# Soft-capped attention ahead of two expert layers: value products of 64 columns, and the sums of the exponentials by additions and one product

## The chip, the core and the metric

The kernel runs on one core of one Trainium2 chip. The metric is the device time of one execution in microseconds, the median of several runs. A profile is taken of one further execution; its span runs from the first to the last instruction. TensorE, VectorE, ScalarE, GpSimd and SyncE are the five engines; the profile calls them PE (PEld for its weight loads), DVE, ACT, POOL and SP, and SPq is SyncE's queue of transfers.

## What is computed

For 2 batches of 12 heads, 448 positions and 64 columns a head:

```
s = (q @ k.T) / sqrt(64)
s = cap * tanh(s / cap)              # cap = 30
a = exp(s - max(s)); a = a / (sum(a) + 1e-9)
x = a @ v                            # heads side by side: 896 tokens x 768
h = x @ w_in;  x = relu(h)**2 @ w_out
h = x @ w_in2; out = (h * clip(h + 3, 0, 6) / 6) @ w_out2
```

Where the cap is at most 40, as here, the kernel leaves the maximum out, since the exponentials can't overflow. It divides after the product with v: the numerator is the product of v and the exponentials, the denominator their sum over the keys.

## The kernel before, in words

There are 12 pairs of heads. Scores are computed transposed, keys on the partitions and the 448 queries along the columns. The 448 keys of a head are three tiles of 128 and a rest of 64; a step handles one key tile g of both heads of a pair: g = 1, 2, 3 the full ones, g = 0 the rest, for which the two heads share the 128 partitions. The stream of 48 steps goes pair by pair in the order `TILES` = 1, 2, 3, 0.

At step t the loop of L362 writes down, in this order, the work of several steps, and each engine takes its own in that order: `scores` (L274: two float32 products of 64 rows, one a head, on the two halves of TensorE's rows), `squash` (L286: ScalarE's tanh out of PSUM, both heads at once), `powers` of the step before (L293: ScalarE's exponential in place) and `weigh` of three steps before (L297, `LAG`). `weigh` multiplies the exponentials by a weight tile of 128 columns: 64 columns of v and 64 of ones, so that one product per head gives numerators in 64 partitions of a bank and, in each of the other 64, the sum. A float32 product shows in the trace as two records.

After a pair's last `weigh`: `evict` copies both banks out on VectorE (L318), and SyncE moves one row of sums for each head to 64 partitions (L319); `invert` adds the guard and takes reciprocals (L324, L325) and SyncE stores the result to DRAM (L327); `spread` has it broadcast to 64 partitions for each head (L333); `divide` multiplies on GpSimd (L340); `part` splits the quotient into a hi part in the fp32r type (GpSimd, L48, for the last pair ScalarE, L46) and a lo part (VectorE, L349), which the expert layers take as `xh` and `xl`. Each of these follows some steps behind the one before. `load` fetches q and k (L234) and v (L272, two transfers a pair into three fixed tiles) three pairs ahead, on SyncE, which issues all transfers in program order and waits where a transfer has to wait.

Spread over the loop, the first three chunks of expert weights are prepared (`split_steps`, five steps a chunk, on GpSimd and VectorE, then the next load, L81). After the loop `begin` starts the first two products of the expert layers (L134): first all that needs batch 0, then batch 1 without the last pair, 66 products in all, and only then what needs the last pair. The expert layers follow on TensorE, three products for each block (hi by hi, hi by lo, lo by hi). Scores take two tiles of two PSUM banks each (`ps_a`), numerators four banks (`ps_o`).

Of the kernel before, what the change touches and what calls it, by code (L numbers as in the profile page):

```python
# [9 lines left out]
F32 = mybir.dt.float32  # L10
# [6 lines left out]
PSUM = bass.MemoryType.PSUM  # L17

B, H, S, D = 2, 12, 448, 64
DM, DFF = 768, 2048  # L20
P = 128
NQ = S // P
REM = S - NQ * P
HP = H // 2
NPAIR = B * HP
# [4 lines left out]
OCH = 4  # L30
NO = KF // OCH
RC = S // D
TILES = (1, 2, 3, 0)
LAG = 3
EPS = 1e-9
SAFE_CAP = 40.0
SAFE_BITS = 0x42200000
# [199 lines left out]
def attention(tc, ex, qk, v, loaded, sc, capt, guard, set_guard):  # L237
# [6 lines left out]
    nc = tc.nc  # L244
    with ExitStack() as actx:
        dram = actx.enter_context(tc.tile_pool(name="dram", bufs=2, space=bass.MemoryType.DRAM))
        a1 = actx.enter_context(tc.tile_pool(name="a1", bufs=1))
        a2 = actx.enter_context(tc.tile_pool(name="a2", bufs=2))
        a3 = actx.enter_context(tc.tile_pool(name="a3", bufs=3))
        a5 = actx.enter_context(tc.tile_pool(name="a5", bufs=5))  # L250
        ps_o = actx.enter_context(tc.tile_pool(name="ps_o", bufs=4, space=PSUM))

        pairs = [{} for _ in range(NPAIR)]
        pairs[0].update(loaded)


        v3 = []
        for i in range(3):
            t = a1.tile([P, NQ + 1, 3, D], F32, name=f"v{i}")
            nc.gpsimd.memset(t[:, :, 1, :], 1.0)  # L260
            v3.append(t)

        def load(p):
            if p >= NPAIR:
                return
            t = pairs[p]
            if p > 0:
                t["qk"] = a3.tile([P, 2, S], F32, name="qk", tag="qk")
                load_qk(nc, t["qk"], qk[p])
            t["v"] = v3[p % 3]  # L270
            for h in range(2):
                nc.sync.dma_start(t["v"][:, :, 2 * h, :], v[p, :, :, h])  # L272

        def scores(p, g):  # L274
            t = pairs[p]
            st = t["st", g] = ex.sums()
            for h in range(2):
                rows = slice(h * D, (h + 1) * D)
                if g:

                    out, c0, n = st[:, h, :S], h * REM + (g - 1) * P, P
                else:
                    out, c0, n = st[rows, 0, :S], (1 - h) * (S - REM), REM
                nc.tensor.matmul(out, t["qk"][rows, 1, c0:c0 + n], t["qk"][rows, 0, :], start=True, stop=True)  # L284

        def squash(p, g):  # L286
            t = pairs[p]
            n = 2 if g else 1
            e = a5.tile([P, 2, S], F32, name="e", tag="e")
            t["e", g] = e[:, :n, :]  # L290
            nc.scalar.activation(t["e", g], t.pop(("st", g))[:, :n, :S], AF.Tanh, scale=sc)  # L291

        def powers(p, g):  # L293
            e = pairs[p]["e", g]
            nc.scalar.activation(e, e, AF.Exp, scale=capt)  # L295

        def weigh(p, g):  # L297
            t = pairs[p]
            e = t.pop(("e", g))
            for h in range(2):  # L300
                if g == TILES[0]:
                    t["po", h] = ps_o.tile([P, 512], F32, name="po", tag="po")
                rows = slice(0, P) if g else slice(h * D, (h + 1) * D)
                w = t["v"][rows, g - 1 if g else NQ, h:h + 2, :].rearrange("p a d -> p (a d)")
                nc.tensor.matmul(  # L305
                    t["po", h][:, :S], w, e[rows, h if g else 0, :],
                    start=g == TILES[0], stop=g == TILES[-1],
                )

        def evict(p):
            t = pairs[p]
            t["ev"] = a2.tile([P, 2, S], F32, name="ev", tag="ev")
            t["rec"] = a2.tile([D, 2, RC], F32, name="rec", tag="rec")
            for h in range(2):
                s0 = (1 - h) * D
                nc.vector.tensor_copy(t["ev"][:, h, :], t.pop(("po", h))[:, :S])  # L318
                nc.sync.dma_start(t["rec"][:, h, :], t["ev"][s0:s0 + 1, h, :].rearrange("o (p c) -> o p c", c=RC))  # L319

        def invert(p):
            t = pairs[p]
            rec = t["rec"]
            nc.vector.tensor_scalar_add(rec, rec, guard[:D])  # L324
            nc.vector.reciprocal(rec, rec)  # L325
            t["rows"] = dram.tile([2, S], F32, name="rows", tag="rows")
            nc.sync.dma_start(t["rows"].rearrange("h (p c) -> p h c", c=RC), rec)  # L327

        def spread(p):
            t = pairs[p]  # L330
            t["rb"] = a2.tile([P, S], F32, name="rb", tag="rb")
            for h in range(2):
                nc.sync.dma_start(t["rb"][h * D:(h + 1) * D], t["rows"][h:h + 1].to_broadcast([D, S]))  # L333

        def divide(p, eng):
            t = pairs[p]
            t["xf"] = a2.tile([P, S], F32, name="xf", tag="xf")
            for h in range(2):
                x = slice(h * D, (h + 1) * D)
                eng.tensor_mul(t["xf"][x], t["ev"][x, h, :], t["rb"][x])  # L340

        def part(p, i, eng):
            xf = pairs[p]["xf"]
            b, hp = divmod(p, HP)
            at = (slice(None), hp, slice(b * S, (b + 1) * S))
            if i == 0:
                copy(nc, eng, ex.xh[at], xf)
            else:
                eng.tensor_sub(ex.xl[at], xf, ex.xh[at].bitcast(F32))  # L349

        load(0)
        set_guard()
        load(1)
        load(2)
        ex.load()
        ex.load()
        stream = [(p, g) for p in range(NPAIR) for g in TILES]
        n, m = len(stream), len(TILES)
        early = (s for w in ("pvp",) * 3 for s in ex.split_steps(w))
        after = {m * (p + 1) - 1 + LAG: p for p in range(NPAIR)}  # L360

        for t in range(n + LAG + 5):  # L362
            if t < n:
                scores(*stream[t])
                squash(*stream[t])
            if 1 <= t <= n:
                powers(*stream[t - 1])
            if LAG <= t < n + LAG:
                weigh(*stream[t - LAG])
            if t in after:  # L370
                evict(after[t])
                load(after[t] + 3)
            if t - 5 in after:
                part(after[t - 5], 1, nc.vector)
            if t - 2 in after:
                invert(after[t - 2])
            if t - 3 in after:
                spread(after[t - 3])
            if t - 4 in after and after[t - 4] < NPAIR - 1:
                divide(after[t - 4], nc.gpsimd)  # L380
                part(after[t - 4], 0, nc.gpsimd)
            elif t - 4 in after:
                divide(after[t - 4], nc.vector)
                part(after[t - 4], 0, nc.scalar)
            if t >= 3 and t % 2:
                next(early, None)
            if t == n:
                for _ in early:
                    pass
        begun = ex.begin([ex.sums() for _ in range(2)])  # L390
        part(NPAIR - 1, 1, nc.vector)
        for _ in begun:
# [144 lines left out]
```

## Time and profile before

| what | value |
|---|---|
| median of 3 runs | 607.37 us (606.34 to 607.92) |
| the profiled execution | 604.25 us, span 602.5 us |
| mean granted TensorE clock | 0.994 of full speed |
| TensorE busy | 587.0 us of the span |
| VectorE, ScalarE, GpSimd busy | 313.3, 276.5 and 156.0 us |
| transfers | 65.14 MB, mean 108 GB/s |

Busy times are shares of one long span with two parts, attention and expert layers, so they don't tell what bounds either; that is read from the timeline. A group of instructions on one line has a count, the busy time, the mean of one, and the idle time of its engine ahead of it with what ended it. In a timeline, consecutive records of a line stand together (x4: four records), with the start and the time to the end of the last; ends on TensorE are modelled, so the distance from start to start tells more than the length.

### The profile page before, as it was taken

What the parts mean: (1) busy time and instruction counts of PE and PEld (TensorE: products, weight loads), DVE (VectorE), ACT (ScalarE), POOL (GpSimd) and SP (SyncE); (2) the same over time, 40 slices, a digit from 0 to 9 for tenths busy, and PEclk for the clock granted to TensorE, in tenths of its full rate; (3) what the DMA queues carried; (4) which work ended last, traced back from release to release, by engine and by line L of the source; (5) the groups of instructions that cost most, each with busy time, mean ns of one, the idle gap of its engine ahead of it and who ended that gap; (6) DMA issues with size and microseconds to landing.
All of it is one profiled execution on the core that took longest, in us unless ns stands there. A gap on an engine that the chain in (4) does not pass through costs nothing.

```text
span 602.5 us, 7241 instructions
## 1 busy us (share of the span) xinstructions
PE 587.0 (97%) x2688; PEld 477.2 (79%) x2688; DVE 313.3 (52%) x423; ACT 276.5 (46%) x434; POOL 156.0 (26%) x123
## 2 busy tenths in 40 slices
PE   6999999997999999999999999999999999999996
PEld 2333333376999999999999999999999999999995
DVE  0333232216766665555555567777777665554430
ACT  6767676705656665422333234555554432222220
POOL 0053433231322222222322232222222132222220
PEclk9999999998999999999999999999999999999998
DMA  7463636102433322234333443333332234433411
GB/s 172 140 157 87 166 77 165 34 17 72 153 106 107 109 92 97 71 106 138 106 105 95 133 156 108 104 106 104 106 110 85 87 104 137 135 115 127 146 57 36
DMA packets 35133, 65.14 MB, mean 108 GB/s; under 512 B 18704, under 2 KB 24848, under 8 KB 35088
## 3 DMA queue, kind: packets, MB, share of 16 engines
q1 hardware_dynamic: 34944, 64.59, 35.4%
q8 instruction: 23, 0.38, 0.2%
q14 instruction: 22, 0.18, 0.1%
q10 hardware_dynamic: 144, 0.00, 0.0%
HBM read 61.74 MB, written 2.80 MB: 107 GB/s over the span
## 4 chain that ended last, share of the span: by engine, by line
PE 81%; DMA 10%; POOL 3%; DVE 2%; issue 1%; SPq 1%; ACT 0%; POOLq 0%; ACTq 0%
PE pm L134 76%; DMA rows<-rec 4%; DMA rb<-rows 4%; PE po L305 3%; POOL xf L340 3%; PE pm L284 3%; DMA qk<-in_qk_dram 1%; DMA rec<-ev 1%; DMA qkfirst<-in_qk_dram 1%; POOL xh L48 1%; SPq L333 0%; DVE rec L325 0%; SPq L319 0%; DVE rec L324 0%; DVE xl L349 0%
## 5 line engine op out<-in xcount | busy, mean ns | idle before, releaser
L108 POOL TENSOR_TENSOR wl<-wv,wh 128x512 fp32r<-128x512 f32 (+1 forms) x80 | 121.2, 1516 | 340.6 <-ACT wh L46 335.7
L98 DVE TENSOR_SCALAR wv<-wy 128x512 uint32<-128x512 uint32 (+1 forms) x80 | 89.8, 1122 | 110.8 <-ACT wy L46 96.5
L134 PE MATMUL pm<-gh,wl 128*128 128x448 f32 x384 | 140.2, 365 | 0.0
L134 PE MATMUL pm<-gl,wh 128*128 128x448 f32 x384 | 140.2, 365 | 0.0
L134 PE MATMUL pm<-gh,wh 128*128 128x448 f32 x384 | 140.2, 365 | 0.0
L46 ACT ACTIVATE wh<-wv 128x512 fp32r<-128x512 f32 (+1 forms) x77 | 54.8, 711 | 106.9 <-PE pm L134 74.4
L134 PEld LDWEIGHTS pm<-gh,wh 128*128 128x128 f32 x384 | 72.1, 188 | 5.7
L134 PEld LDWEIGHTS pm<-gl,wh 128*128 128x128 f32 x384 | 72.1, 188 | 5.7
L134 PEld LDWEIGHTS pm<-gh,wl 128*128 128x128 f32 x384 | 72.1, 188 | 5.7
L134 PE MATMUL pm<-xh,wh 128*128 128x448 f32 x192 | 71.1, 370 | 3.3 <-ACT xh L46 3.3
L305 PE MATMUL po<-e,v 128*128 128x448 f32 (+1 forms) x192 | 74.2, 558 | 0.0
L134 PE MATMUL pm<-xl,wh 128*128 128x448 f32 x192 | 71.0, 370 | 1.0 <-DVE xl L349 1.0
L134 PE MATMUL pm<-xh,wl 128*128 128x448 f32 x192 | 70.8, 369 | 0.0
L134 PE MATMUL pm<-yh,wh 128*128 128x448 f32 x192 | 70.1, 365 | 0.0
L134 PE MATMUL pm<-yl,wh 128*128 128x448 f32 x192 | 70.1, 365 | 0.0
L134 PE MATMUL pm<-yh,wl 128*128 128x448 f32 x192 | 70.1, 365 | 0.0
L100 DVE SCALAR_TENSOR_TENSOR wv<-wr,wv 128x512 uint32<-128x512 uint32 (+1 forms) x80 | 63.8, 798 | 2.7
L102 DVE SCALAR_TENSOR_TENSOR wv<-wy,wv 128x512 uint32<-128x512 uint32 (+1 forms) x80 | 63.7, 796 | 2.6
L305 PEld LDWEIGHTS po<-e,v 128*128 128x128 f32 (+1 forms) x192 | 29.1, 188 | 41.6 <-issue 30.1
L291 ACT ACTIVATE e<-pm,sc 128x896 f32<-128x896 f32 (+1 forms) x48 | 43.8, 911 | 32.2 <-PE pm L284 32.2
L46 ACT ACTIVATE wy<-wr 128x512 f32<-128x512 f32 (+1 forms) x77 | 56.9, 739 | 1.8 <-DMA wr<-in_wo_dram 1.6
L295 ACT ACTIVATE e<-e,capt 128x896 f32<-128x896 f32 (+1 forms) x48 | 45.0, 940 | 0.0
(45 smaller groups left out, 512.7 us busy)
## 6 DMA issues: line engine op xcount, KB each, us to landing
wr<-in_wi_dram SPq DMA_DIRECT2D x32, 768.0 KB, 4.4
wr<-in_wo_dram SPq DMA_DIRECT2D x48, 512.0 KB, 3.5
qk<-in_qk_dram SPq DMA_DIRECT2D x22, 224.0 KB, 3.8
v<-in_v_dram SPq DMA_DIRECT2D x24, 128.0 KB, 3.7
rb<-rows SPq DMA_DIRECT2D x24, 112.0 KB, 2.8
out_dram<-o SPq DMA_DIRECT2D x12, 224.0 KB, 2.0
qkfirst<-in_qk_dram SPq DMA_DIRECT2D x2, 224.0 KB, 4.1
rec<-ev SPq DMA_DIRECT2D x24, 1.8 KB, 2.2
```

The costliest lines, as they stand in the source:

```text
L46: eng.activation(dst, src, AF.Copy, scale=scale)
L48: eng.tensor_scalar(dst, src, scale, 1.0, op0=ALU.mult, op1=ALU.mult)
L98: nc.vector.tensor_scalar(w, y, 3, None, op0=ALU.logical_shift_left)
L100: nc.vector.scalar_tensor_tensor(w, low, 29, w, op0=ALU.logical_shift_right, op1=ALU.bitwise_or)
L102: nc.vector.scalar_tensor_tensor(w, y, 0x80000000, w, op0=ALU.bitwise_and, op1=ALU.bitwise_or)
L108: by[2].tensor_sub(l, w.bitcast(F32), h.bitcast(F32))
L134: self.nc.tensor.matmul(ps[:, b, :S], w[:, k - k0, :], a[:, k, b * S:(b + 1) * S], start=(k == 0 and w is wh and a is ah), stop=(k == nk - ...
L284: nc.tensor.matmul(out, t["qk"][rows, 1, c0:c0 + n], t["qk"][rows, 0, :], start=True, stop=True)
L291: nc.scalar.activation(t["e", g], t.pop(("st", g))[:, :n, :S], AF.Tanh, scale=sc)
L295: nc.scalar.activation(e, e, AF.Exp, scale=capt)
L305: nc.tensor.matmul(t["po", h][:, :S], w, e[rows, h if g else 0, :], start=g == TILES[0], stop=g == TILES[-1],)
L340: eng.tensor_mul(t["xf"][x], t["ev"][x, h, :], t["rb"][x])
```

## The change

Value products get weight tiles of 64 columns (v alone), one product for each head, into the two halves of the partitions of one bank instead of two banks. The exponentials of a pair's key tiles are added up on VectorE (`add`), and one product per head with a tile of ones (`total`) sums the result over the partitions, in a bank of its own, into 64 equal rows. `evict` copies only these sums. `divide` is one VectorE instruction that reads the numerators from PSUM; the hi part is on ScalarE for all pairs. A pair's v comes in one transfer. The loop now goes by rounds of one pair, with the work of neighbouring rounds written between.

```diff
@@ -247,18 +245,16 @@
         a1 = actx.enter_context(tc.tile_pool(name="a1", bufs=1))
         a2 = actx.enter_context(tc.tile_pool(name="a2", bufs=2))
         a3 = actx.enter_context(tc.tile_pool(name="a3", bufs=3))
-        a5 = actx.enter_context(tc.tile_pool(name="a5", bufs=5))
-        ps_o = actx.enter_context(tc.tile_pool(name="ps_o", bufs=4, space=PSUM))
+        a4 = actx.enter_context(tc.tile_pool(name="a4", bufs=4))
+        a8 = actx.enter_context(tc.tile_pool(name="a8", bufs=8))
+        ps_o = actx.enter_context(tc.tile_pool(name="ps_o", bufs=3, space=PSUM))
+        ps_t = actx.enter_context(tc.tile_pool(name="ps_t", bufs=1, space=PSUM))
 
...
-        v3 = []
-        for i in range(3):
-            t = a1.tile([P, NQ + 1, 3, D], F32, name=f"v{i}")
-            nc.gpsimd.memset(t[:, :, 1, :], 1.0)
-            v3.append(t)
+        halves = [slice(h * D, (h + 1) * D) for h in range(2)]
+        ones = a1.tile([P, D], F32, name="ones")
+        nc.gpsimd.memset(ones, 1.0)
 
         def load(p):
             if p >= NPAIR:
@@ -267,15 +263,13 @@
             if p > 0:
                 t["qk"] = a3.tile([P, 2, S], F32, name="qk", tag="qk")
                 load_qk(nc, t["qk"], qk[p])
-            t["v"] = v3[p % 3]
-            for h in range(2):
-                nc.sync.dma_start(t["v"][:, :, 2 * h, :], v[p, :, :, h])
+            t["v"] = a4.tile([P, NQ + 1, 2, D], F32, name="v", tag="v")
+            nc.sync.dma_start(t["v"], v[p])
 
...
         def squash(p, g):
             t = pairs[p]
             n = 2 if g else 1
-            e = a5.tile([P, 2, S], F32, name="e", tag="e")
-            t["e", g] = e[:, :n, :]
+            t["e", g] = a8.tile([P, 2, S], F32, name="e", tag="e")[:, :n, :]
             nc.scalar.activation(t["e", g], t.pop(("st", g))[:, :n, :S], AF.Tanh, scale=sc)
 
         def powers(p, g):
@@ -296,27 +289,44 @@
 
         def weigh(p, g):
             t = pairs[p]
-            e = t.pop(("e", g))
-            for h in range(2):
-                if g == TILES[0]:
-                    t["po", h] = ps_o.tile([P, 512], F32, name="po", tag="po")
-                rows = slice(0, P) if g else slice(h * D, (h + 1) * D)
-                w = t["v"][rows, g - 1 if g else NQ, h:h + 2, :].rearrange("p a d -> p (a d)")
+            if "po" not in t:
+                t["po"] = ps_o.tile([P, 512], F32, name="po", tag="po")
+            for h, half in enumerate(halves):
+                rows, at = (slice(0, P), h) if g else (half, 0)
                 nc.tensor.matmul(
-                    t["po", h][:, :S], w, e[rows, h if g else 0, :],
-                    start=g == TILES[0], stop=g == TILES[-1],
+                    t["po"][half, :S], t["v"][rows, g - 1 if g else NQ, h, :], t["e", g][rows, at, :],
+                    start=g == 1, stop=g == 0,
                 )
 
 
+        def add(p, g, eng):
+            t = pairs[p]
+            if g == 2:
+                t["es"] = a2.tile([P, 2, S], F32, name="es", tag="es")
+                eng.tensor_add(t["es"], t["e", 1], t["e", 2])
+            elif g:
+                eng.tensor_add(t["es"], t["es"], t["e", g])
+            else:
+                for h, half in enumerate(halves):
+                    eng.tensor_add(t["es"][half, h, :], t["es"][half, h, :], t["e", 0][half, 0, :])
+
+        def total(p):
+            t = pairs[p]
+            t["pt"] = ps_t.tile([P, 512], F32, name="pt", tag="pt")
+            for h, half in enumerate(halves):
+                nc.tensor.matmul(t["pt"][half, :S], ones, t["es"][:, h, :], start=True, stop=True)
+
+
 
         def evict(p):
             t = pairs[p]
-            t["ev"] = a2.tile([P, 2, S], F32, name="ev", tag="ev")
+            t["tot"] = a2.tile([P, S], F32, name="tot", tag="tot")
+            nc.vector.tensor_copy(t["tot"], t.pop("pt")[:, :S])
             t["rec"] = a2.tile([D, 2, RC], F32, name="rec", tag="rec")
             for h in range(2):
-                s0 = (1 - h) * D
-                nc.vector.tensor_copy(t["ev"][:, h, :], t.pop(("po", h))[:, :S])
-                nc.sync.dma_start(t["rec"][:, h, :], t["ev"][s0:s0 + 1, h, :].rearrange("o (p c) -> o p c", c=RC))
+                nc.sync.dma_start(
+                    t["rec"][:, h, :], t["tot"][h * D:h * D + 1, :].rearrange("o (p c) -> o p c", c=RC)
+                )
 
         def invert(p):
             t = pairs[p]
@@ -329,15 +339,13 @@
         def spread(p):
             t = pairs[p]
             t["rb"] = a2.tile([P, S], F32, name="rb", tag="rb")
-            for h in range(2):
-                nc.sync.dma_start(t["rb"][h * D:(h + 1) * D], t["rows"][h:h + 1].to_broadcast([D, S]))
+            for h, half in enumerate(halves):
+                nc.sync.dma_start(t["rb"][half], t["rows"][h:h + 1].to_broadcast([D, S]))
 
         def divide(p, eng):
             t = pairs[p]
             t["xf"] = a2.tile([P, S], F32, name="xf", tag="xf")
-            for h in range(2):
-                x = slice(h * D, (h + 1) * D)
-                eng.tensor_mul(t["xf"][x], t["ev"][x, h, :], t["rb"][x])
+            eng.tensor_mul(t["xf"], t.pop("po")[:, :S], t["rb"])
 
         def part(p, i, eng):
             xf = pairs[p]["xf"]
@@ -348,45 +356,50 @@
             else:
                 eng.tensor_sub(ex.xl[at], xf, ex.xh[at].bitcast(F32))
 
+        def on(p, step, *args):
+            if 0 <= p < NPAIR:
+                step(p, *args)
+
         load(0)
         set_guard()
         load(1)
         load(2)
         ex.load()
         ex.load()
-        stream = [(p, g) for p in range(NPAIR) for g in TILES]
-        n, m = len(stream), len(TILES)
         early = (s for w in ("pvp",) * 3 for s in ex.split_steps(w))
-        after = {m * (p + 1) - 1 + LAG: p for p in range(NPAIR)}
-
-        for t in range(n + LAG + 5):
-            if t < n:
-                scores(*stream[t])
-                squash(*stream[t])
-            if 1 <= t <= n:
-                powers(*stream[t - 1])
-            if LAG <= t < n + LAG:
-                weigh(*stream[t - LAG])
-            if t in after:
-                evict(after[t])
-                load(after[t] + 3)
-            if t - 5 in after:
-                part(after[t - 5], 1, nc.vector)
-            if t - 2 in after:
-                invert(after[t - 2])
-            if t - 3 in after:
-                spread(after[t - 3])
-            if t - 4 in after and after[t - 4] < NPAIR - 1:
-                divide(after[t - 4], nc.gpsimd)
-                part(after[t - 4], 0, nc.gpsimd)
-            elif t - 4 in after:
-                divide(after[t - 4], nc.vector)
-                part(after[t - 4], 0, nc.scalar)
-            if t >= 3 and t % 2:
+
+        for r in range(NPAIR + 2):
+            on(r - 2, invert)
+            on(r - 2, spread)
+            for g in (1, 2):
+                on(r, scores, g)
+                on(r, squash, g)
+            for g in (1, 2):
+                on(r, powers, g)
+            on(r - 1, add, 3, nc.vector)
+            on(r - 1, add, 0, nc.vector)
+            on(r - 1, weigh, 2)
+            on(r - 1, weigh, 3)
+            on(r - 1, total)
+            on(r - 3, part, 1, nc.vector)
+            on(r - 1, evict)
+            load(r + 3)
+            for g in (3, 0):
+                on(r, scores, g)
+                on(r, squash, g)
+            for g in (3, 0):
+                on(r, powers, g)
+            on(r, add, 2, nc.vector)
+            on(r - 1, weigh, 0)
+            on(r, weigh, 1)
+            if 0 < r < NPAIR:
                 next(early, None)
-            if t == n:
+                next(early, None)
+            if r == NPAIR:
                 for _ in early:
                     pass
+            on(r - 2, divide, nc.vector)
+            on(r - 2, part, 0, nc.scalar)
         begun = ex.begin([ex.sums() for _ in range(2)])
         part(NPAIR - 1, 1, nc.vector)
         for _ in begun:
```

## Rows read from the trace of the kernel before

**Rows 1.** The page, busy time, share of the span and instructions of each engine.

```profile
PE 587.0 (97%) x2688; PEld 477.2 (79%) x2688; DVE 313.3 (52%) x423; ACT 276.5 (46%) x434; POOL 156.0 (26%) x123
```

**Rows 2.** Windows: stretch and length, PE, PEld, DVE, ACT, POOL, clock, transfers.

```profile
140.00:160.00 20.00, 19.12 (x85) 17.36 (x86) 16.53 (x20) 15.02 (x28) 5.55 (x3) 0.91 0.35 119
160.00:300.00 140.00, 140.00 (x692) 129.72 (x692) 82.50 (x100) 67.98 (x127) 35.36 (x23) 1.00 0.32 103
```

**Rows 3.** Timeline of TensorE, one pair in attention: start, length, line, tiles.

```profile
51.05 1.02 PE L284 MATMUL pm<-qk 64*128 64x448 f32 x4
52.00 1.77 PE L305 MATMUL po<-e,v 128*128 128x448 f32 x4
53.70 1.02 PE L284 MATMUL pm<-qk 64*128 64x448 f32 x4
...
56.35 1.02 PE L284 MATMUL pm<-qk 64*128 64x448 f32 x4
57.21 0.92 PE L305 MATMUL po<-e,v 64*128 64x448 f32 x4
58.06 0.97 PE L284 MATMUL pm<-qk 64*64 64x448 f32 x4
58.96 1.77 PE L305 MATMUL po<-e,v 128*128 128x448 f32 x4
60.66 1.02 PE L284 MATMUL pm<-qk 64*128 64x448 f32 x4
```

**Rows 4.** Timeline of ScalarE at the start, where it works without a gap.

```profile
10.73 1.00 ACT L291 ACTIVATE e<-pm,sc 128x896 f32<-128x896 f32 x1
11.62 1.04 ACT L295 ACTIVATE e<-e,capt 128x896 f32<-128x896 f32 x1
12.56 0.63 ACT L291 ACTIVATE e<-pm,sc 128x448 f32<-128x448 f32 x1
13.07 1.04 ACT L295 ACTIVATE e<-e,capt 128x896 f32<-128x896 f32 x1
```

**Rows 5.** Groups by form, VectorE: busy us, mean ns, idle before.

```profile
L100 DVE SCALAR_TENSOR_TENSOR wv<-wr,wv 128x512 uint32<-128x512 uint32 x48 | 33.2, 692 | 1.6
L100 DVE SCALAR_TENSOR_TENSOR wv<-wr,wv 128x768 uint32<-128x768 uint32 x32 | 30.6, 955 | 1.0
L318 DVE COPY ev<-po 128x448 f32<-128x448 f32 x24 | 13.8, 616 | 21.2 <-PE po L305 21.2
L340 DVE TENSOR_TENSOR xf<-ev,rb 64x448 f32<-64x448 f32 x2 | 1.2, 620 | 4.8 <-DMA rb<-rows 4.7
```

**Rows 6.** Timeline of SyncE's queue, issues of transfers: start, time to issue.

```profile
38.31 0.58 SPq L81 DMA_DIRECT2D wr<-in_wi_dram  x1
39.59 1.12 SPq L319 DMA_DIRECT2D rec<-ev  x2
...
51.74 1.23 SPq L272 DMA_DIRECT2D v<-in_v_dram  x2
55.36 0.64 SPq L327 DMA_DIRECT2D rows<-rec  x1
```

**Rows 7.** Transfers: count, KB each, median us from issue to landing.

```profile
rb<-rows SPq DMA_DIRECT2D x24, 112.0 KB, 2.8
...
rec<-ev SPq DMA_DIRECT2D x24, 1.8 KB, 2.2
rows<-rec SPq DMA_DIRECT2D x12, 3.5 KB, 2.3
```

**Rows 8.** Timeline of TensorE at the seam to the expert layers.

```profile
122.28 0.47 PE L134 MATMUL pm<-xh,wh 128*128 128x448 f32 x1
...
136.36 0.36 PE L134 MATMUL pm<-xh,wl 128*128 128x448 f32 x1
140.03 0.47 PE L134 MATMUL pm<-xh,wh 128*128 128x448 f32 x1 [3.31 <-ACT xh L46]
...
145.24 0.37 PE L134 MATMUL pm<-xh,wh 128*128 128x448 f32 x1
```

**Rows 9.** Chain of work that ended last, 38 to 46 us: start, length.

```profile
39.59 4.70 DMA rec<-ev
```

More of the change, by code (lines that the diff above doesn't have):

```diff
@@ L32 @@
 RC = S // D
-TILES = (1, 2, 3, 0)
-LAG = 3
 EPS = 1e-9
@@ L276, in scores @@
             st = t["st", g] = ex.sums()
-            for h in range(2):
-                rows = slice(h * D, (h + 1) * D)
+            for h, rows in enumerate(halves):
                 if g:
@@ L337, in divide @@
             t["xf"] = a2.tile([P, S], F32, name="xf", tag="xf")
-            for h in range(2):
-                x = slice(h * D, (h + 1) * D)
-                eng.tensor_mul(t["xf"][x], t["ev"][x, h, :], t["rb"][x])
+            eng.tensor_mul(t["xf"], t.pop("po")[:, :S], t["rb"])
         def part(p, i, eng):
```

## The prediction

> **What bounds the kernel now.** I read the page first: TensorE is busy for 97% of the span [rows 1], so a change pays where it shortens TensorE's queue or removes a hole in it. The windows then split the span. From 160 us on TensorE is full and takes 692 products in 140 us, 0.202 us each [rows 2]; these are the expert layers, which the diff leaves alone. What can move is attention, up to about 141 us, and the seam behind it.
>
> The timeline of TensorE shows attention's beat [rows 3]. I call a score product of key tile g Sg and a value product Wg; each stands for both heads. One pair of heads runs S, W, S, W, S, W0, S0, W in 9.61 us (51.05 to 60.66). S to W takes 0.95 us and W to S 1.70: the two heads' 64-row products (4 records, L284) pass side by side, the two 128-row ones of L305 one after the other. Without a change of shape a side-by-side group is 0.86 (56.35 to 57.21), even for W0, which has 64 rows. So a change of shape costs about 0.09 to 0.2 us, and the three full W groups take 5.1 of the 9.61 us. Attention is bound by TensorE, not by ScalarE, whose waits are for scores.
>
> The seam: the first expert products start at 122.28 and run to 136.36; then TensorE waits for the last pair's quotient until 140.03, and products come at full pace again only from 145.24 [rows 8]. The granted clock is 0.91 over 140 to 160 us [rows 2], so part of that stretch ran at 1.2 GHz behind the hole. 78 products x 0.202 = 15.8 us took 22.96: the seam costs 7.2 us.
>
> **The change, part by part.**
>
> *Value products.* Each W (g = 1 to 3) becomes two products of 128 rows by 64 columns, one per head, into the two halves of one bank. No row shows two such products together. Lower bound for a group: 0.75, two records at a time of 4 in 1.50 (1.70 less the 0.2 of the change of shape). Upper bound: 1.50, one after the other as now. I take 0.86, the price of the 64-row groups, since these differ in rows and columns and yet pass together: S0 and its successor follow at 0.85 and 0.90 [rows 3]. The Trainium skill ("TensorE: Matmul & The Clock Gate", Part 3) speaks for less: three column tiles side by side gained 2.38, not 3. By that a group would be, as an estimate, 1.50 / (2 x 0.79) = 0.95, and the sum below 4 us worse; no run here shows it yet.
>
> *The sums* add one group T, two products of 128 by 64 again: 0.86.
>
> *A round now* is S1 0.86, S2 0.95, W2 0.86, W3 0.86, T 0.95, S3 0.86, S0 0.85, W0 0.90, W1 0.95: 8.04 us against 9.61, with 0.95 where the shape changes next.
>
> *ScalarE* is the next bound to check. Start to start, a tanh of 896 columns takes 0.89, an exponential 0.94, a tanh of 448 0.51 [rows 4]; with the small exponential and the hi part at no more than 0.66 each, a round has 3 x 0.89 + 3 x 0.94 + 0.51 + 1.32 = 7.3 us. It fits, with 0.7 us to spare.
>
> *VectorE* takes on the additions. The 896-column one has no row; 512 columns took 0.692 and 768 0.955 with two inputs, so 1.09 by that slope [rows 5]; at least 0.955, at most double the 512-column price, 1.38. Two of these, two half additions at 0.62, one copy instead of two at 0.62, the quotient from PSUM at 0.62, the lo part at 0.62 and the inversion below one such pass: 5.9 us. Weight preparation adds up to two steps of 0.955 in the first eight rounds: 7.8. It fits, barely. T waits for the last additions, but S1, S2, W2 and W3 (3.5 us) cover the 2.3 us of them; in the last round there are no scores and T waits some 0.8 us. GpSimd loses its quotient and hi part and keeps weight steps: nothing on the path.
>
> *SyncE.* A pair has one value load instead of two. The load of pair r + 3 now waits for round r's S0 and W0, so it stands right ahead of the next inverted sums' transfer; before, that came 3.6 us behind the value load [rows 6]. Bounds: nothing, or the whole of a load's transfer. Ahead of a late one the trace has its price: sums issued 1.3 us behind a weight load landed after 4.70 us [rows 6, 9] instead of the usual 2.2 [rows 7]. Three weight loads fall into attention; I take 1 us of stall for each, since the 2.5 us extra meet about 1.5 us of slack in the quotient at the round's end: 3 us.
>
> *The attention sum.* Tanh and exponential swap places at the start: S1 of pair 1 waits for the third tanh, which now takes the slot of 11.62 to 12.56 [rows 4], so it starts at 12.6. Eleven rounds of 8.04 end at 101.0; the last, W2, W3, wait, T, W0, is 0.86 + 0.86 + 0.8 + 0.95 + 0.95 = 4.4. Expert products would start at 105.4 instead of 122.28: 16.9 us sooner.
>
> *The seam.* From the end of T the last pair needs copy 0.62, sums 0.55 + 2.2, inversion 0.5, store 2.3, broadcast 0.55 + 2.8, quotient 0.62, hi 0.58, lo 0.64: 11.4 us [rows 5, 7]. The 66 products that need nothing of it last 66 x 0.202 = 13.3 and start 0.95 behind T. So the hole closes, and with it the low clock: of 7.2 us I leave 1 for gaps and gain 6.2. What speaks the other way is the queue: before, the last sums stood behind the pair before on SyncE, and may again.
>
> Sum: 16.9 + 6.2 - 3 = 20.1 us. The profiled execution took 604.25 (span 602.5), 3.1 below the median of 607.37; off the median this gives **587 us**.
>
> **The rivals.**
>
> *A, column products don't pass together* (slower). For it: no row has two products that share all 128 rows, and every 128-row group here runs in turn. Against: groups sharing neither rows nor bank halves pass together. At 1.50 a group a round is 8.04 + 4 x 0.64 = 10.60; the last, without a wait, 1.5 + 1.5 + 1.6 + 0.95 = 5.6. Experts start at 12.6 + 116.6 + 5.6 = 134.8, 12.5 later than now; less 6.2 of the seam that is 6.3 slower, **614**. It decides from a group price of 1.30: each 0.1 above 0.86 costs 4 x 11.5 x 0.1 = 4.6 us, and 20.1 us hold 4.4 such steps.
>
> *B, the round trip of the sums sets the round.* Copy, sums, inversion, store and broadcast are chained across rounds, since SyncE waits for the store to land ahead of each broadcast, and the next pair's sums queue behind. A turn is inversion 0.5, store 2.3, broadcasts 1.1, sums 1.1 + 1.65 and gaps 0.2, 6.85 us: under 8.04. If one small transfer in each turn lands in 4.70, it is 9.35. Then eleven rounds are 14.4 longer, less the 3 already counted, and a hole of 1 to 3 us stays: **600**. For it: loads of 700 KB a pair now stand ahead of the store. The Trainium skill ("DMA: Bandwidth & Descriptors", Queues, rings and completion order) says the transfers of one issuing engine share its rings on the same 16 engines and are taken in ring order, which would make this the rule in every round; the row of 4.70 agrees. Against: rows 7 show a median of 2.3 for the store with loads under way.
>
> *C, groups cheaper than I take*, at 0.75, and no late landings: 4 x 0.11 x 11.5 + 3 + 1 = 9 more gained, **578**.
>
> **How the numbers follow.** Forecast 0.68 (580 to 594), C 0.04, B 0.11, A 0.14, and 0.03 for something that leaves it within 0.3% (1.8 us), about what a measurement of this kernel can tell from no change. The range reaches from C to B with a few us for its seam, 578 to 603, and leaves A out. Faster by over 0.3%: 0.68 + 0.04 + 0.11 = 0.83; within: 0.03; slower: 0.14.
>
> **What would show it.** In the timeline of the changed kernel the two records of W1 to W3 should start together and a group follow the next at 0.86 to 0.95; a pair should take about 8.0 us, with ScalarE waiting less for scores. No hole of 3 us between the 66th expert product and the next, and a granted clock of 1.00 there. Groups at 1.5 would mean A. VectorE idle ahead of the inversion for landed sums, with TensorE idle ahead of T, would mean B. Expert layers at another pace than 0.202 us a product would make the whole account wrong.

## The result and the profile after

The changed kernel took **593.08 us** (median of 4 runs, 589.56 to 593.88) beside 607.22 (606.34 to 607.92) of the kernel before on the same chip: a ratio of 0.9757, 95% interval 0.9714 to 0.9799. It is faster, as forecast, and inside the range; but the forecast was 587, so of the 20.1 us promised 14.1 came in the medians. In the two profiled spans it is 602.5 - 592.1 = 10.4 us, mostly since the profiled execution of the kernel before (604.25) lies 3.0 us below its median; that of the changed kernel (593.88) lies 0.8 above its own. In all comparisons below, runs in which the chip was some per cent slower throughout are left out; the profiles of experiments 4, 7 and 12 are of such runs, but their clean rounds take the usual 7.6 us.

The page's busy times, against [rows 1]:

```profile
PE 571.3 (96%) x2736; PEld 464.6 (78%) x2736; DVE 354.2 (60%) x468; ACT 280.7 (47%) x445; POOL 124.8 (21%) x88
```

The windows answer to [rows 2], with two rounds of attention, a stretch of the second of them and the seam ahead (stretch, length, PE, PEld, DVE, ACT, POOL, clock, share and GB/s of transfers):

```profile
66.37:73.98 7.61, 7.61 (x38) 2.43 (x36) 6.35 (x9) 7.24 (x11) 0.00 (x0) 1.00 0.64 195
73.98:86.70 12.72, 10.07 (x38) 2.90 (x36) 7.40 (x14) 7.36 (x11) 1.82 (x1) 0.87 0.36 96
82.00:84.00 2.00, 2.00 (x6) 0.70 (x8) 1.99 (x3) 0.38 (x2) 0.00 (x0) 0.50 0.25 92
...
120.00:140.00 20.00, 20.00 (x100) 18.53 (x99) 8.58 (x13) 8.57 (x17) 1.86 (x1) 1.00 0.16 52
140.00:160.00 20.00, 20.00 (x101) 18.53 (x100) 15.86 (x19) 15.03 (x27) 6.03 (x4) 1.00 0.47 159
160.00:300.00 140.00, 140.00 (x693) 129.73 (x692) 82.22 (x100) 63.76 (x119) 35.65 (x24) 1.00 0.30 98
```

The expert layers go on at 140 / 693 = 0.202 us a product. At the seam 100 products fill 20 us at a clock of 1.00: the hole of [rows 8] and its 7.2 us are gone. So of the 10.4 us the seam gave 7.2 and attention only 3.2, where 16.9 less 3 were forecast for it. The two rounds in the windows show why: one takes 7.61 us, the other 12.72, and in that one TensorE was idle for 2.65 us and its mean granted clock was 0.87.

TensorE's timeline of these two rounds, against [rows 3]:

```profile
66.37 1.77 PE L278 MATMUL pm<-qk 64*128 64x448 f32 x8
68.07 1.72 PE L296 MATMUL po<-e,v 128*64 128x448 f32 x8
69.63 0.92 PE L317 MATMUL pt<-es,ones 128*64 128x448 f32 x4
70.48 1.92 PE L278 MATMUL pm<-qk 64*128 64x448 f32 x8
72.23 1.82 PE L296 MATMUL po<-e,v 64*64 64x448 f32 x8
73.98 1.77 PE L278 MATMUL pm<-qk 64*128 64x448 f32 x8
75.69 1.72 PE L296 MATMUL po<-e,v 128*64 128x448 f32 x8
80.06 1.92 PE L317 MATMUL pt<-es,ones 128*64 128x448 f32 x4 [2.65 <-DVE es L311]
81.91 3.22 PE L278 MATMUL pm<-qk 64*128 64x448 f32 x8
84.96 1.82 PE L296 MATMUL po<-e,v 64*64 64x448 f32 x8
86.70 1.77 PE L278 MATMUL pm<-qk 64*128 64x448 f32 x8
```

In the first round W2 and W3 together take 1.56 us from start to start (68.07 to 69.63). W2 follows a group of another shape and takes 0.80; W3, which follows its like, takes 0.75 (from 68.87), half of the 1.50 that the two heads' products took in turn: they do pass side by side. In the second, T (L317) stands 2.65 us for the additions, then lasts 1.0 longer than in the first round (some 0.7 because its second product waits as well, as at 51.48, where T takes 1.62 at full clock, and the rest by the clock, which fell at 81.24), and the next group takes 3.22 instead of 1.92: behind the idle time the clock was at 0.50, the lower level of 1.2 GHz (the window of 82 to 84 us). These three, 5.0 us, are the whole difference of the two rounds (5.1).

VectorE's and SyncE's timelines of the same stretch say why the additions were late:

```profile
73.25 0.96 DVE L100 SCALAR_TENSOR_TENSOR wv<-wy,wv 128x768 uint32<-128x768 uint32 x1
77.31 0.62 DVE L348 TENSOR_TENSOR xf<-po,rb 128x448 f32<-128x448 f32 x1 [3.10 <-DMA rb<-rows]
77.85 0.22 DVE L334 TENSOR_SCALAR rec<-rec,guard 64x14 f32<-64x14 f32 x1
78.10 0.23 DVE L335 RECIPROCAL rec<-rec 64x14 f32<-64x14 f32 x1
78.26 1.02 DVE L308 TENSOR_TENSOR es<-es,e 128x896 f32<-128x896 f32 x1
79.38 1.27 DVE L311 TENSOR_TENSOR es<-es,e 64x448 f32<-64x448 f32 x2
```

```profile
66.16 0.53 SPq L267 DMA_DIRECT2D v<-in_v_dram  x1
66.74 0.43 SPq L79 DMA_DIRECT2D wr<-in_wi_dram  x1
67.34 0.63 SPq L337 DMA_DIRECT2D rows<-rec  x1
73.90 1.12 SPq L343 DMA_DIRECT2D rb<-rows  x2
```

The chain of waits has the store between them, against 2.3 in [rows 7]:

```profile
67.34 6.54 DMA rows<-rec
```

The store of the inverted sums was issued right behind a weight load of 768 KB and landed after 6.54 us; only then could the broadcast go, and VectorE, which takes its instructions in order, stood 3.10 us at the quotient with the additions queued behind it. The other two weight loads in attention have stores of 6.44 us behind them. The first of these two has a second long round in its wake (9.83 us after 10.39): its late broadcast holds up the next pair's sums on SyncE, and the next inversion waits 1.38 us for them. All six waits of T in attention (us in total, times, longest):

```profile
PE pt L317 <- DVE es L311: 9.3, 6, 2.6
```

The ten rounds from 12.88 to 107.02 us take 94.1 us; at 7.62 each they would take 76.2. These 17.9 us are what attention lost again.

### The profile page after: what moved, and what is told of

Same layout as the page of the kernel before. It is cut to its first block, busy times and chain, and to the rows that moved or that the text cites. A ratio compares the mean times of both kernels' runs of the same rounds, so it can differ in the third digit from the quotient of the medians.

```text
span 592.1 us, 7324 instructions
## 1 busy us (share of the span) xinstructions
PE 571.3 (96%) x2736; PEld 464.6 (78%) x2736; DVE 354.2 (60%) x468; ACT 280.7 (47%) x445; POOL 124.8 (21%) x88
## 4 chain that ended last, share of the span: by engine, by line
PE 86%; DMA 8%; DVE 3%; ACT 1%; SPq 1%; issue 0%; POOL 0%; DVEq 0%; ACTq 0%
PE pm L132 79%; DMA rows<-rec 4%; PE pm L278 3%; DMA rb<-rows 2%; PE po L296 2%; PE pt L317 2%; DVE es L308 1%; DMA rec<-tot 1%; DMA qkfirst<-in_qk_dram 1%; ACT e L288 1%; DVE es L311 1%; ACT e L284 1%; SPq L343 1%; POOL wl L106 0%; DVE xf L348 0%
## 5 line engine op out<-in xcount | busy, mean ns | idle before, releaser
L284 ACT ACTIVATE e<-pm,sc 128x896 f32<-128x896 f32 (+1 forms) x48 | 41.5, 909 | 14.4 <-PE pm L278 14.3
L278 PE MATMUL pm<-qk 64*128 64x448 f32 (+1 forms) x176 | 43.4, 602 | 0.9 <-ACT e L284 0.9
L288 ACT ACTIVATE e<-e,capt 128x896 f32<-128x896 f32 (+1 forms) x48 | 42.7, 941 | 0.0
L296 PE MATMUL po<-e,v 128*64 128x448 f32 (+1 forms) x192 | 42.4, 551 | 0.0
```

Source lines behind the costliest of these rows:

```text
L296: nc.tensor.matmul(t["po"][half, :S], t["v"][rows, g - 1 if g else NQ, h, :], t["e", g][rows, at, :], start=g == 1, stop=g == 0,)
```

## The experiments

**1. Weight loads from another queue.**

```diff
+        ex.wq = nc.scalar
...
-        self.nc.sync.dma_start(raw[:, :n * P, :]..., src...)
+        self.wq.dma_start(raw[:, :n * P, :]..., src...)
```

> The changed kernel, with the three weight loads that fall into attention issued from ScalarE's queue instead of SyncE's. Theory (queue): the store of the inverted sums lands after 6.4 us in the three rounds behind a weight load only because it stands behind that load in SyncE's queue. Then the store lands within 4 us in every round, rounds of 10.4, 12.7 and 12.7 us fall to 7.6 to 8.5, and the time is 577 to 583. Rival (traffic): the load fills the shared transfer engines whoever issues it, the store still lands after 5 us or more, and the time is 589 to 594. Rival (VectorE): the weight steps on VectorE delay the additions; moving the loads changes nothing, 591 to 594.

588.24 to 590.06 us, ratio 0.9641 (0.9546 to 0.9735). The stores of the three rounds still landed after 5.3 to 6.0 us, T still waited up to 2.0. With the queue changed, most of the lateness stays. (The Trainium skill, "DMA: Bandwidth & Descriptors", Issuing engines are not separate DMA queues, says that transfers of all engines interleave on the same 16 engines; 6.0 instead of 6.5 us agrees.)

**2. No weight load in attention.** The third chunk is loaded at the start into a tile of its own, the fourth and fifth behind the last broadcast.

```diff
+        ex.load(a1)
+        ex.hold = True
...
+        ex.hold = False
+        ex.load()
+        ex.load()
```

> The changed kernel, with no weight load inside the rounds: the third chunk is loaded ahead of the loop into a tile of its own, the fourth and fifth behind the last broadcast. The weight steps on VectorE and GpSimd stay where they are. Theory (queue) and rival (traffic) both expect the long landings gone and 577 to 584, with up to 2 us lost at the start to one more load there and nothing at the seam. Rival (VectorE): 591 to 594, with rounds of 10 us and more still there. Together with the kernel that changes only the queue it separates queue from traffic.

582.14 to 584.58 us, ratio 0.9532 (0.944 to 0.9624); no store took over 3.6 us, and the experts started at 109.29 instead of 119.09 us. So the late stores behind weight loads cost some ten microseconds. What is left is a round of 11 us at the start, where the load went, and one of 9.4 in which VectorE's 64x14 addition took 1.12 us instead of 0.22 and an addition 1.63 instead of 1.02.

**3. No round trip.** VectorE adds the guard and inverts all 128 x 448 equal sums out of PSUM, and the three transfers of a pair are left out.

```diff
+            nc.vector.tensor_scalar_add(t["rb"], t.pop("pt")[:, :S], guard)
+            nc.vector.reciprocal(t["rb"], t["rb"])
...
-            on(r - 2, invert)
-            on(r - 2, spread)
```

> The changed kernel without the transfers of the sums: since the product with ones gives the sum in all 64 partitions of a head, VectorE adds the guard out of PSUM and takes the reciprocal on 128 x 448 directly. The reciprocal of 14 columns took 0.233 us and of 1 column 0.165, 5.2 ns a column, so about 2.4 us for 448. VectorE then has 2.2 + 1.3 + 0.6 + 2.4 + 0.6 + 0.6 = 7.7 us a round, and up to 9.6 in the rounds with two weight steps. Theory (the round trip through SyncE's queue is what stalls): no round is over 10 us, none shows the clock falling, the long ones are set by VectorE at 8 to 9.6 us, 583 to 591. Rival (something else than the round trip makes the rounds of 12.7 us): they stay, 593 or more.

602.51 to 604.21 us, ratio 0.9864 (0.9769 to 0.9959): a miss. The group of this reciprocal on VectorE:

```profile
L325 DVE RECIPROCAL rb<-rb 128x448 f32<-128x448 f32 x11 | 32.5, 2953 | 0.4
```

At 2.95 us a pair VectorE is busy for 74.1 of the 80 us from 30 to 110, TensorE for 67.6, and T waits up to 3.4 us for its additions; rounds grew to 12 us. The run can't price the round trip, but it shows how little room VectorE has.

**4. All loads of the rounds from GpSimd's queue.**

```diff
+        ex.wq = nc.gpsimd
...
+                load_qk(nc.gpsimd if p > 2 else nc.sync, t["qk"], qk[p])
...
+            (nc.gpsimd if p > 2 else nc.sync).dma_start(t["v"], v[p])
```

> The changed kernel, with all large loads inside the rounds (q and k, v, weights) issued from GpSimd's queue; SyncE keeps the sums, the store and the broadcast alone. Theory (queue): no small transfer stands behind a large one, landings are 1.9 to 2.8 us, every round is 7.6 to 7.9 us as the undisturbed ones of the changed kernel, and the time is 574 to 579, some 3 us below the kernel that moves the weight loads alone. Rival (traffic): landings stay above 3 us in most rounds, 583 to 594.

590.68 us (one run). The stores behind weight loads landed sooner, after 3.5 to 4.7 us, so the queue has a part in the lateness; yet the time hardly fell, so its order isn't the whole cause. The timeline shows something else in a long round, VectorE's tiny addition of the guard beside GpSimd's subtraction of 768 columns:

```profile
38.23 2.75 DVE L335 TENSOR_SCALAR rec<-rec,guard 64x14 f32<-64x14 f32 x1
...
38.66 1.83 POOL L107 TENSOR_TENSOR wl<-wv,wh 128x768 fp32r<-128x768 f32 x1
```

2.75 us for an operation that takes 0.22 elsewhere. (In this run GpSimd also issues loads, at 38.07 and 40.43, right ahead of the subtraction and right behind it, so the 2.75 is not the subtraction's alone.) That made a second suspect.

**5. Additions first.** Only the order: inversion, quotient and lo part go behind the additions and T, the quotient a round later; the store comes ahead of the loads on SyncE.

```diff
-        for r in range(NPAIR + 2):
-            on(r - 2, invert)
-            on(r - 2, spread)
+        for r in range(NPAIR + 3):
...
             on(r - 1, total)
-            on(r - 3, part, 1, nc.vector)
+            on(r - 2, invert)
+            on(r - 3, divide, nc.vector)
+            on(r - 4, part, 1, nc.vector)
             on(r - 1, evict)
+            on(r - 2, spread)
             load(r + 3)
...
-            on(r - 2, divide, nc.vector)
-            on(r - 2, part, 0, nc.scalar)
+            on(r - 3, part, 0, nc.scalar)
```

> The changed kernel, with another order on VectorE and SyncE and nothing else: in each round the last additions of the pair before come first, then the inversion, and the quotient a round later; SyncE issues store, sums, broadcast. All loads and weight steps stay. Theory (order): a late landing costs time only because the inversion and the quotient stand ahead of the next additions on VectorE, which works in order, and the product of the sums waits for these. Then the store may still land after 6 us behind a weight load, but TensorE waits for no additions from the second round on, rounds are 7.6 to 8.5 us, the clock stays at full speed and the time is 576 to 583. Rival (traffic): late transfers hold up rounds through the loads of q, k and v, rounds of 10 us and more stay, 588 to 594.

579.61 to 581.07 us, median 580.19, ratio 0.9459 (0.9402 to 0.9515). The timeline of TensorE, one round and the first expert product, and T's waits in attention:

```profile
61.01 1.77 PE L278 MATMUL pm<-qk 64*128 64x448 f32 x8
...
68.62 1.77 PE L278 MATMUL pm<-qk 64*128 64x448 f32 x8
...
104.15 0.47 PE L132 MATMUL pm<-xh,wh 128*128 128x448 f32 x1
```

```profile
PE pt L317 <- DVE es L311: 1.1, 2, 0.6
```

The ten rounds from 12.67 to 92.13 us are 3.3 over 76.2 instead of 17.9, the waits 1.1 instead of 9.3, and the experts start 14.9 us sooner than in the changed kernel. The stores behind weight loads land after 3.7 to 4.8 us here, so this run alone doesn't show what a later one would cost; experiment 11 does.

**6. The same without GpSimd's subtractions** (on VectorE instead).

```diff
-        early = (s for w in ("pvp",) * 3 for s in ex.split_steps(w))
+        early = (s for w in ("pvv",) * 3 for s in ex.split_steps(w))
```

> As the kernel with the additions first, and the three subtractions that make the low halves of the first weight chunks on VectorE instead of GpSimd. Theory (GpSimd in the way): while GpSimd subtracts, VectorE's instructions run long (additions of 1.6 us instead of 1.0, tiny ones of 0.6 to 2.8 us instead of 0.2); then no addition is over 1.15 us here and the time is 0.5 to 3 us below the kernel that has only the additions first. Rival (VectorE full): three more passes of 0.95 us on VectorE cost as much as they save, within 1 us of it.

578.26 to 581.02 us, ratio 0.9441 (0.9382 to 0.9499): no difference from 5 that can be measured. The stretched additions of 896 columns (2.62 us at the longest in 5) are gone (1.09); two half additions of 1.12 and 1.23 instead of 0.62 are left, beside GpSimd's other weight step. The stretched ones cost next to nothing there.

**7. The changed kernel with that edit alone.**

```diff
-        early = (s for w in ("pvp",) * 3 for s in ex.split_steps(w))
+        early = (s for w in ("pvv",) * 3 for s in ex.split_steps(w))
```

> The changed kernel in its own order, with only the three subtractions moved from GpSimd to VectorE. Theory (queue and order set the long rounds): the three rounds behind weight loads stay at 10 to 13 us, the time falls by at most 3 us, 589 to 593. Rival (GpSimd in the way is the main cost): all rounds fall below 9 us, 580 to 585.

590.73 to 592.49 us. The guard's addition is short again (0.227 at most), yet T still waits 2.17, 2.34 and 2.15 us in three rounds. GpSimd's subtraction is a real disturbance and not the main cause.

**8. All three:** additions first, subtractions on VectorE, no weight load in the rounds (the edits of 2, 5 and 6 together).

```diff
...
+        ex.load(a1)
+        ex.hold = True
+        early = (s for w in ("pvv",) * 3 for s in ex.split_steps(w))
```

> The changed kernel with three of the edits together: additions first, the subtractions of the weights on VectorE, no weight load inside the rounds. If each long round has one of the causes shown so far, all rounds from the third on are 7.6 to 7.8 us, expert products start at 103 to 106 us and the time is 574 to 579. If it is no faster than the kernel with the additions first alone, late landings cost nothing once the additions don't stand behind them.

577.59 to 578.32 us, median **578.0**, ratio 0.942 (0.9364 to 0.9476): the fastest of all, and 2 us below 5 on the same chip. TensorE's timeline now repeats (start to start 7.62 us), to the first expert product:

```profile
67.55 1.77 PE L279 MATMUL pm<-qk 64*128 64x448 f32 x8
...
75.17 1.77 PE L279 MATMUL pm<-qk 64*128 64x448 f32 x8
...
102.41 0.47 PE L133 MATMUL pm<-xh,wh 128*128 128x448 f32 x1
```

**9. The kernel before with the quotient off GpSimd:** VectorE divides and ScalarE makes the hi part for every pair; nothing else of the change.

```diff
-            if t - 4 in after and after[t - 4] < NPAIR - 1:
-                divide(after[t - 4], nc.gpsimd)
-                part(after[t - 4], 0, nc.gpsimd)
-            elif t - 4 in after:
+            if t - 4 in after:
                 divide(after[t - 4], nc.vector)
                 part(after[t - 4], 0, nc.scalar)
```

> The kernel before, with one part of the change alone: quotient and hi part of every pair on VectorE and ScalarE instead of GpSimd (the quotient still from the copies in SBUF). Theory (column products carry the gain of the rounds, the seam is a matter of the queues): the pair stays at 9.61 us, experts start at 122 us as before, and only the chain of the last pair gets shorter, by the 2 us that the pair before it saves on GpSimd, of which the hole at the seam gives back 1 to 3 us: 604 to 606 where the kernel before shows 607. Rival (GpSimd's quotient held the attention rounds up): rounds under 9.3 us and 600 or less.

598.02 to 599.12 us, ratio 0.9871 (0.9844 to 0.9898), 7.6 us below the kernel before: more than expected. Rounds stay at 9.61 us and the experts start at 124.25, later than in [rows 8], yet the window of the seam has no hole of 3 us:

```profile
120.00:140.00 20.00, 19.63 (x90) 15.90 (x89) 9.26 (x17) 5.53 (x11) 0.00 (x0) 1.00 0.11 25
```

GpSimd and VectorE in the kernel before, ahead of the hole:

```profile
129.29 2.36 POOL L340 TENSOR_TENSOR xf<-ev,rb 64x448 f32<-64x448 f32 x2 [6.26 <-DMA rb<-rows]
131.73 0.57 POOL L48 TENSOR_SCALAR xh<-xf 128x448 fp32r<-128x448 f32 x1
132.33 0.63 DVE L349 TENSOR_TENSOR xl<-xf,xh 128x448 fp32r<-128x448 f32 x1 [7.24 <-POOL xh L48]
132.88 0.22 DVE L324 TENSOR_SCALAR rec<-rec,guard 64x14 f32<-64x14 f32 x1
```

VectorE's last inversion stands in order behind the lo part of the pair before, which waits for GpSimd's quotient and hi part (2.36 and 0.57 us). With these on VectorE and ScalarE:

```profile
128.95 0.22 DVE L324 TENSOR_SCALAR rec<-rec,guard 64x14 f32<-64x14 f32 x1
```

The inversion starts at 128.95 instead of 132.88 us. So the seam hung on GpSimd, and about half of the change's gain in the medians can be had from this part alone.

**10. One head's products, then the other's.** Does the pairing hang on the order of issue?

```diff
-        def weigh(p, g):
+        def weigh(p, g, heads=(0, 1)):
...
-            on(r - 1, weigh, 2)
-            on(r - 1, weigh, 3)
+            for h in range(2):
+                on(r - 1, weigh, 2, (h,))
+                on(r - 1, weigh, 3, (h,))
```

> The kernel with the additions first, with only the order of four products changed: in the groups W2 and W3 both products of one head come first, then both of the other, so that a product follows one on the same half of the columns. Theory (two products of 64 columns run side by side only next to each other on different halves): the six products W2, W3, T take four lengths of 0.75 us instead of three side-by-side groups, 0.75 to 0.85 us more a round, some 9 us in all: 587 to 591. Rival (a product of 64 columns costs half a product of 128 wherever it stands): 579 to 582.

580.69 to 582.82 us, ratio 0.9587 (0.9559 to 0.9616), beside 580.19 for 5 on another chip. TensorE's timeline:

```profile
47.12 1.73 PE L297 MATMUL po<-e,v 128*64 128x448 f32 x8
48.67 0.93 PE L318 MATMUL pt<-es,ones 128*64 128x448 f32 x4
```

W2 and W3 still take 1.55 us: products on one half of the columns run beside later ones on the other half. The miss speaks for halves that work independently. (The Trainium skill, "TensorEngine Tiling (Array Packing)", Key Properties, says that tiles operate independently; the rows agree.)

**11. Experiment 5 with the weight load ahead of the store again.**

```diff
             on(r - 1, total)
+            if 0 < r < NPAIR:
+                next(early, None)
+                next(early, None)
             on(r - 2, invert)
...
             on(r, weigh, 1)
-            if 0 < r < NPAIR:
-                next(early, None)
-                next(early, None)
```

> The kernel with the additions first, with the two weight steps of a round moved ahead of the inversion, so that the weight load is again issued right ahead of the store on SyncE. Theory (order on VectorE): the store lands after more than 5 us in three rounds, and it costs next to nothing, since neither inversion nor quotient stands ahead of the additions: 578 to 583, no wait of TensorE for additions over 1 us. Rival (the gain of the kernel with the additions first came from the store's new place on SyncE): rounds of 10 us and more come back, 585 to 593.

580.86 and 581.36 us (two runs). SyncE's queue and T's waits in attention:

```profile
58.47 0.42 SPq L79 DMA_DIRECT2D wr<-in_wi_dram  x1
59.00 0.63 SPq L337 DMA_DIRECT2D rows<-rec  x1
...
64.72 1.10 SPq L343 DMA_DIRECT2D rb<-rows  x2
```

```profile
PE pt L317 <- DVE es L311: 1.2, 2, 0.7
```

The stores behind weight loads are nearly as late as in the changed kernel (5.7 to 6.4 us from issue to landing), and it costs about nothing. The quotient still waits for broadcasts, up to 2.54 us (at 84.17), and no T waits over 0.7: a late landing costs time where the additions stand behind it on VectorE. The edit of 5 changes two things there: the additions stand ahead of the quotient, and the quotient gets a round more, which shortens its waits (2.9 to 4.9 us behind late stores in the changed kernel). How much of the gain is the one and how much the other is not separated.

**12. One head only:** experiment 5 without the second head's products of key tiles 2 and 3, so that part of the numerators is left out.

```diff
-            for h, half in enumerate(halves):
+            for h, half in list(enumerate(halves))[:1 if g in (2, 3) else 2]:
```

> The kernel with the additions first, with the second head's products of the key tiles 2 and 3 left out (so the second head's numerators lack these tiles); all else, the additions and sums too, stays. Theory (the two heads' products of 64 columns run side by side, each as long as a product of 128): leaving one of each out saves nothing; the groups W2 and W3 still take 1.5 us together up to T, the round stays at 7.62 us and the time at 578 to 582. Rival (a product of 64 columns takes half the time and the two run in turn): the two groups take 0.8 us, TensorE's round falls below ScalarE's, and the time is 574 to 577.

580.08 us (one run). TensorE's timeline of one round's value products and T, to the scores behind them:

```profile
46.79 1.34 PE L296 MATMUL po<-e,v 128*64 128x448 f32 x3
47.69 0.59 PE L317 MATMUL pt<-es,ones 128*64 128x448 f32 x1
47.97 0.54 PE L296 MATMUL po<-e,v 128*64 128x448 f32 x1
48.12 1.14 PE L317 MATMUL pt<-es,ones 128*64 128x448 f32 x3
49.19 1.92 PE L278 MATMUL pm<-qk 64*128 64x448 f32 x8
```

From W2's start to the scores 2.40 us, as with both heads (2.41 in 5). Leaving one head's products out saves nothing: they had passed beside the other's. (A record of T, at 47.69, even starts ahead of the last one of W3, at 47.97.)

## Why the prediction was right in sign and wrong in size

- **The step that failed** is the term for SyncE: "Three weight loads fall into attention; I take 1 us of stall for each". The place was right, the size was not. It took its price from a transfer of 4.70 us [rows 9], where the same trace has one of 5.61 behind another weight load (the sums issued at 89.64); the store took 6.44 to 6.54. It let 2.5 us of lateness meet 1.5 us of slack at the quotient; it did not follow what stands behind the quotient on VectorE, where the next round's additions wait, and behind those T. Instead of 3 us, ten rounds lost 17.9: 1.3 in the first, 1.5 in the third and fourth, and 15.2 in the three behind late stores and the one in the wake of the first, of which some 3 by the clock at 1.2 GHz (2.8 of it in one group each, 3.22 and 3.38 instead of 1.92). Less the 4.2 that cheaper groups gave (below) that is 13.7 us, by which the experts started later than forecast (119.09 for 105.4). Experiments 5 and 11 show this cause: with the additions first about 580 us, in 11 with the store nearly as late.
- **Rival B** named that round trip, at 9.35 us in every round and 600 us. It decided in four rounds of the ten, at 9.8 to 12.7 us. Three are TensorE's, at 7.61 to 7.62; three more lost 0.6 to 1.3 us, where T's second product waited for additions. Its sign, VectorE idle ahead of the inversion, came to 1.38 us at most in these rounds; the longer idle times stood ahead of the quotient (2.9 to 4.9 us).
- **The groups** were taken at 0.86 and cost 0.75, the lower bound, as **rival C** had it; with the groups of another shape a clean round is 7.62 us, not 8.04. The 0.86 was misread as a price without a change of shape: the group at 56.35 [rows 3] follows one of another shape and holds some 0.1 for it. The estimate of 0.95, worked out from the Trainium skill's figure for three column tiles ("TensorE: Matmul & The Clock Gate", Part 3), erred to the other side; here the measurement decides. This hid part of the failed term: ten rounds at 0.42 less are 4.2 us, so the forecast came nearer to the time than its terms did, by luck. Experiment 8, with groups at 0.75 and no late stores, gives 578.0 us, C's figure, though by another order of instructions.
- **Rival A** is excluded by the groups' 0.75, and by 12: where one head's products are left out, the stretch takes as long.
- **The seam** gave the whole 7.2 us where 6.2 were taken. The chain of the last pair took 11.2 us (118.30 to 129.5 on the timeline of VectorE) for a forecast of 11.4, ahead of the first product that needs it, some 132.4. But that the hole was the quotient's on GpSimd in the kernel before, and so could be closed without the rest, is shown only by 9.
- **VectorE's prices** held: 1.09 us for an 896-column addition (forecast 1.09), 1.27 for the two halves (1.24). "It fits, barely" was right for the sum of its work, and missed that an engine that works in order needs room at the right place.
- With all loads in place, 5 reaches the expert layers at 104.15 us, near the 105.4 that the forecast had ahead of its 3 us of stalls, and 8 at 102.41.

Experiment 1's 4.5 us in the span (587.6 for 592.1) are all in attention (the experts start at 114.64): T waits 6.4 us instead of 9.3, and there is one stretch of attention at a clock of 0.50 instead of two. Not separated: how much of the 2 us between 5 and 8 is the loads and how much the subtractions (6 says mostly the loads, within its spread), and, in 5, the order on VectorE from the round that the quotient gains.

## What to carry to other kernels

Where one engine in order serves both the bound engine and a chain of transfers, put what waits for a transfer behind what the bound engine waits for, even at the price of one more round; here late transfers then cost next to nothing (experiment 11). Price a small transfer by the slowest landing beside a large load that the trace has, and follow what stands behind its wait. Before crediting a large change with a closed hole, look for the one instruction that held it open; moving that alone may close it.

## What was not expected of the hardware

- A 3.5 KB store, 2.3 us in the median before, took 6.4 to 6.5 us right behind a load of 768 KB in its own queue, 5.3 to 6.0 with that load issued from ScalarE's queue, and 3.5 to 4.7 with all loads on GpSimd's.
- While GpSimd subtracted 768 columns, VectorE's 64x14 addition took up to 1.12 us instead of 0.22 (experiment 2) and an 896-column addition 2.62 instead of 1.09 (experiment 5):

```profile
51.85 1.82 POOL L106 TENSOR_TENSOR wl<-wv,wh 128x768 fp32r<-128x768 f32 x1 [13.12 <-DVE wh L48]
51.99 2.62 DVE L308 TENSOR_TENSOR es<-es,e 128x896 f32<-128x896 f32 x1 [0.23 <-ACT e L288]
```

  (The Trainium skill, "SBUF — State Buffer", SBUF: two separate sides, tells of a port pair that the two engines hold in turn for a whole instruction. These rows agree: the addition ends 0.95 us behind the subtraction. With the subtraction on VectorE, in 6 and 7, no 896-column addition was stretched.)
- TensorE's wait of 2.65 us was followed by a granted clock of 0.50, which cost another 1.3 us in the next group. So was one of 2.00 us in experiment 1, but not one of 2.57 in experiment 2.
